# A gated convolution with a mixture of experts on one core: the second unit's weights asked for behind the first rows, and the last group's digits, root and logit differences put between the steps of its ranks

## The chip, the cores and the metric

The kernel runs on one core of one Trainium2 chip. The metric is the device time of one execution in microseconds (us). Before the change three runs took 562.46, 561.94 and 562.39 us, a median of 562.39. An execution was also profiled; all rows of the trace below are from that one.

The names of the engines in the profile: PE is TensorE (matmuls; PEld its weight loads), DVE is VectorE, ACT is ScalarE, POOL is GpSimd, SP is SyncE, which issues most DMA transfers. A trailing q (SPq) marks what an engine's sequencer issues.

## What is computed

```python
def reference(A_q, A_k, A_v, A_shift_k, A_ssm_k, A_ssm_D, B_x, B_wg, B_w1, B_w2):
    x = A_q                                           # 1 x 2048 x 512
    h = x + _A_ref(_layernorm(x), A_k, A_v, A_shift_k, A_ssm_k, A_ssm_D)
    return h + _B_ref(_layernorm(h), B_wg, B_w1, B_w2)

def _B_ref(x, wg, w1, w2):                            # 8 experts, one for each token
    gates = _softmax(xt @ wg)
    topk_idx = jnp.argsort(-gates, -1)[:, :1]
    topk_g = gate of that expert, divided by itself
    h = _gelu(jnp.einsum("nd,edf->nef", xt, w1))      # w1: 8 x 512 x 1792
    y = jnp.einsum("nef,efd->ned", h, w2)             # w2: 8 x 1792 x 512
    return sum over experts of (its weight) * y
```

`_A_ref` is a short and a long causal convolution per channel (the long one by a Fourier transform), with gates. Only the expert that a token chose is computed.

## The kernel before

**Phase 1** makes h, in 16 groups of 128 tokens, writes its rows to `hrow` in memory, and routes: logits, the chosen expert of each token, and the token's rank in its expert. The routing goes in four groups g of 4 times 128 tokens. For each: `pick_steps` (the greatest logit, a one-hot `ohe`, counts `cum`), `rank_own` (two matmuls), `rank_steps` (six dependent instructions on DVE that give the rank and its slot), `route_slots` (one-hot rows `oneb` of the slots), `val_digits` (mean and inverse deviation of a token cut in three bf16 digits `dig`, by four instructions), `rank_select` (`sel`), `route_digits` (`rhs`, the digits times `sel`) and `index_digits` (`rhsj`). `route_list(g)` are the matmuls that sort the digits into lists by slot (`pi`), `route_index` those that sort the row numbers.

**The hand-over to phase 2** is `last_rows`, then `last_group` (group 3), then lines 1762 to 1773. The expert with the most tokens so far, the leader, is computed first; it is known from the first three groups (`leader_steps`, its number in `whol`). Its rows come in three tiles: tile 0 of 128 rows from the first three groups (row numbers `idxa`), tiles 1 (128) and 2 (56 used) behind group 3 (row numbers `idxe`). `gather_rows` (L912) fetches a tile from `hrow` by an indirect DMA on POOL. `first_center` (L973) subtracts the mean and scales on DVE (`xf`), `turn` in `first_in` transposes on PE (L987, `px`), ACT casts to `xh`, DVE takes the rest `xl`, and `multiply` (L1001) starts the first layer: xh by w0h, xh by w0l, xl by w0h, for tile 0 and the first half of the unit's columns, then the rest (128x184), then the second half (128x312).

**Weights.** A unit j is 256 of an expert's 1792 inner columns, 7 units to an expert. `weight_load(j, (0,))` asks SP for its block of w1 (512 KB, L881), `weight_load(j, (1,))` for that of w2 (L884); `weight_cast` (ACT, L899) and `weight_sub` (DVE, L905) split it into w0h, w0l or w1h, w1l. `phase2` puts loads behind a small transfer `seen` (L1445) that reads one row of a gathered tile, and so waits on SP until the tile has landed: the first group of loads behind tile 0, the second behind tile 1.

**What sets the order.** Each engine runs its instructions in program order; in this part the order is written out by hand. `weave` takes one step of each list in turn. Semaphores make an engine wait for another. `spin` (L483, counts in `SPIN`) issues matmuls on a tile of ones that nobody reads; keys c, d, e, f, h, i stand in this part. `values_load` (L876) reads a number from memory into SP's registers, and checks its bounds there unless told not to.

Of the kernel before, what the change touches and what calls it, by code (L numbers as in the profile page):

```python
# [15 lines left out]
AF = mybir.ActivationFunctionType  # L16
# [5 lines left out]
P = 128  # L22
# [59 lines left out]
PAIRS = (1, 3, 5, 7, 9, 11, 13, 15)  # L82
SPLIT = PAIRS[:6]
POOLED = (0, 2, 4, 6, 8, 10)
SPIN = dict(s=24, g=8, a=12, f=14, i=3, h=3, c=12, d=3, e=5)


LAGS = dict(A=0, T=2, L=4)
# [40 lines left out]
class Kernel:  # L129
# [595 lines left out]
    def leader_steps(self):  # L725
        nc, rp = self.nc, self.rp
        key = rp.tile([P, E], F32, name="keyl")
        yield nc.vector.scalar_tensor_tensor(key, self.pl0, float(E), self.tie, op0=ALU.mult, op1=ALU.add)
        top = self.top
        yield nc.vector.tensor_reduce(top, key, axis=AX.X, op=ALU.max)  # L730
        self.lead = rp.tile([P, E], F32, name="lead")
        yield nc.vector.tensor_tensor(self.lead, key, top.to_broadcast([P, E]), op=ALU.is_equal)
        yield nc.vector.tensor_tensor(self.leadp, key, top.to_broadcast([P, E]), op=ALU.is_equal)
        rows = self.lead_rows(0, 12)
        yield next(rows)
        who = rp.tile([P, E], F32, name="whol")
        yield nc.vector.tensor_mul(who, self.lead, self.iotp[:, :E])
        yield next(rows)
        at = rp.tile([P, 1], F32, name="at")
        yield nc.vector.tensor_reduce(at, who, axis=AX.X, op=ALU.add)  # L740
        self.whol = rp.tile([P, 1], I32, name="wholi")
        yield nc.vector.tensor_scalar_sub(self.whol, at, 1.0)

    def route_list(self, g):
        nc, one, rhs = self.nc, self.oneb[:, 4 * g:4 * g + 4], self.rhs[g]
# [47 lines left out]
    def route_exp(self):  # L793
        nc = self.nc
        lg = self.lg
        nc.vector.tensor_sub(lg[:, 12:], self.plg[3][:, :, 0], self.bc(self.mx[:, 12:]))
        nc.vector.tensor_mul(lg, lg, self.val[:, :, 2].unsqueeze(2).to_broadcast([P, N2, E]))

    def route_weights(self):
        nc, rp, lg, mx = self.nc, self.rq, self.lg, self.mx  # L800
# [71 lines left out]
    def weight_load(self, j, parts=(0, 1)):  # L872
        nc = self.nc
        e, c = divmod(j, NJ)
        if c == 0 and 0 in parts:
            self.eid = nc.values_load(self.who[0:1, e:e + 1] if e else self.whol[0:1, 0:1], engines=[mybir.EngineType.SP],  # L876
                                      min_val=0, max_val=E - 1)
        w1, w2 = self.w1[ds(self.eid, 1)], self.w2[ds(self.eid, 1)]
        if 0 in parts:
            r = self.rawt[j, 0] = self.raw.tile([P, DC, FB * P], F32, name="raw1")  # L880
            nc.sync.dma_start(r, w1.rearrange("o (p b) f -> p (o b) f", p=P)[:, :, c * FB * P:(c + 1) * FB * P])  # L881
        if 1 in parts:
            r = self.rawt[j, 1] = self.raw.tile([P, FB, D], F32, name="raw2")
            nc.sync.dma_start(r, w2.rearrange("o (b p) d -> p (o b) d", p=P)[:, c * FB:(c + 1) * FB, :])  # L884
# [91 lines left out]
    def first_in(self):  # L976

        nc = self.nc
        hi, lo = self.xt[0] = self.split(self.xp, self.ident, "x", 2, [P, DC, CAPS[0]])
        tiles = self.first_tiles()  # L980
        ps = [self.px.tile([P, 512], F32, name="px").rearrange("p (c n) -> p c n", c=DC) for _ in tiles][::-1]

        def turn(t):
            n = tiles[t].stop - tiles[t].start
            xv = self.xs[t].rearrange("p (d c) -> p c d", c=DC)
            for b in range(DC):
                nc.tensor.transpose(ps[t][:, b, :n], xv[:n, b, :], self.ident[:n, :n])  # L987
            nc.scalar.copy(hi[:, :, tiles[t]], ps[t][:, :, :n])

        def low(t):  # L990
            n = tiles[t].stop - tiles[t].start
            nc.vector.tensor_sub(lo[:, :, tiles[t]], ps[t][:, :, :n], hi[:, :, tiles[t]].bitcast(F32))

        self.plt = [self.pl1.tile([P, 512], F32, name=f"pl{f}", bufs=1) for f in range(FB)]
        pl = [p[:, :CAPS[0]] for p in self.plt]
        wh, wl = self.wt[0, 0]

        def multiply(s, f, i):
            w, x = ((wh, hi), (wl, hi), (wh, lo))[i]
            for b in range(DC):  # L1000
                nc.tensor.matmul(pl[f][:, s], w[:, b, f * P:(f + 1) * P], x[:, b, s],  # L1001
                                 start=i + b == 0, stop=i == 2 and b == DC - 1)

        rest = slice(P, CAPS[0])
        turn(0)
        self.slot_consts()
        self.spin("e", self.pd)
        self.first_center(2)
        low(0)
        multiply(tiles[0], 0, 0)  # L1010
        multiply(tiles[0], 0, 1)
        turn(1)
        turn(2)
        multiply(tiles[0], 0, 2)
        self.weight_cast(1, 0)
        self.weight_cast(0, 1)
        low(1)
        low(2)
        for i in range(3):
            multiply(rest, 0, i)  # L1020
        for i in range(3):
            multiply(slice(0, CAPS[0]), 1, i)
        return pl
# [306 lines left out]
    def last_rows(self):  # L1330
# [29 lines left out]
        self.rank_sum(2)  # L1360
        self.logits(14)
        weave(self.leader_steps(), self.rank_steps(2))
        for j in range(2):
            self.weight_load(j, (0,))
        self.route_slots(2, dve)
        self.index_digits(1, pool)
        self.route_digits(1, pool)
        self.val_digits(2, pool)
        self.logits(15)

    def last_group(self):
# [6 lines left out]
        self.spin("a", self.psT)  # L1378
        self.ahead_index()
        self.lead_index(0, 12)  # L1380
        self.rank_select(2)
        self.index_digits(2, pool)
        next(pick)
        next(pick)
        self.ahead_rows()
# [4 lines left out]
            self.tc.add_manual_dep(ready.ins, x.name, mybir.DependencyInfo(mybir.DependencyClass.Sync, mybir.DependencyReason.DATA),  # L1390
                                   reason="rows kept and read before they are gathered")
        self.first = [self.gather_rows(self.xp, self.idxa, P)]
        self.route_digits(2, pool)
        self.rank_own(3)
        self.spin("f", self.psT)
        weave(self.rank_steps(3), self.lead_rows(12, N2))
        self.route_slots(3, dve, 0, 2)
        self.lead_digits(12, N2)
        self.route_slots(3, dve, 2, 4)
        self.lead_index(12, N2)  # L1400
        self.ahead_digits()
        self.lead_rows_index()
        self.first_gather()
        self.spin("i", None)
        self.ahead_values()
        self.spin("h", None)
        self.route_scale(3)
        self.val_digits(3, dve, range(1))
        self.route_exp()
        nc.scalar.activation(self.lg, self.lg, AF.Exp)  # L1410
        nc.scalar.activation(self.warm, self.eps, AF.Gelu_apprx_tanh)
        self.val_digits(3, dve, range(1, 4))
        self.rank_select(3)
        self.route_list(1)
        self.route_list(2)
        self.route_digits(3, dve)
        self.index_digits(3, dve)
        self.spin("c", None)
        self.route_list(3)
        self.route_index()  # L1420
        self.hp.release()
        self.open_weights()
        self.weight_cast(0, 0)

    def open_experts(self):
        tc, R = self.tc, self.RIGHT
# [13 lines left out]
    def phase2(self):  # L1440
        nc, tc = self.nc, self.tc
        self.spin("d", self.pd)
        for t, units in enumerate((((0, 1),), ((2, 0), (1, 1), (2, 1), (3, 0), (3, 1), (4, 0), (4, 1)))):
            seen = tc.dram_tile([1, D], F32, name=f"seen{t}")
            gate = nc.sync.dma_start(seen, self.first[t][0:1])  # L1445
            with tc.issue_after(gate.ins):
# [380 lines left out]
```

## Time and profile before

| what | us |
|---|---|
| median of three runs | 562.39 |
| the profiled execution, device time | 561.27 |
| its span, first to last instruction | 559.3 |
| PE busy in the span | 547.8 |
| DVE busy | 450.3 |
| ACT busy | 342.9 |
| POOL busy | 261.7 |
| last steps of the routing and first rows, about | 205 to 224 |

Times in the trace are us from the span's start. In a timeline a row is start, duration, engine, line, operation, result<-inputs, shapes and a count; brackets hold the idle time of the engine before it, and what ended that. A row of the view of waits is total us, times, longest. A row of the view by stretches is busy share (instructions) of PE, PEld, DVE, ACT and POOL, the granted clock of TensorE, the busy share of the DMA engines, and GB/s.

### The profile page before, as it was taken

The numbers are of one execution on the slowest core, as the hardware profiler recorded it, in microseconds if no ns is written. First come the engines' busy times: TensorE is split into PE (matmuls) and PEld (weight loads), VectorE is DVE, ScalarE is ACT, GpSimd is POOL, SyncE is SP. The second block draws the span as 40 slices with busy tenths as digits, with TensorE's granted clock in tenths as the row PEclk, the third lists the DMA queues.
The fourth block names the chain that finished last, engine by engine and source line by source line (L and its number), as shares of the span: only waits on it lengthen the run. The fifth ranks groups of instructions, "written<-read, shape, count | busy, mean of one in ns | idle before, by whom it ended". The sixth has DMA issues, their size and how long they took to land. (4 is left out here: it accounts for less than half of the span.)

```text
span 559.3 us, 10976 instructions
## 1 busy us (share of the span) xinstructions
PE 547.8 (98%) x3753; PEld 471.3 (84%) x3754; DVE 450.3 (81%) x839; ACT 342.9 (61%) x577; POOL 261.7 (47%) x264
## 2 busy tenths in 40 slices
PE   8999999999999998999999999999999999999995
PEld 7857675766556787999999999999999999898984
DVE  5886977889989798878987789899788788786751
ACT  2485667644677753765656566667667667666651
POOL 1055425711367783065574868456457367300201
PEclk9999999999999999999999999999999999999998
DMA  8964559485502326998665767687687778776401
GB/s 320 367 180 179 152 172 377 130 298 154 148 1 94 111 99 181 331 254 297 184 189 169 227 191 217 185 242 232 202 232 211 228 213 284 226 226 200 156 2 38
DMA packets 62674, 110.49 MB, mean 198 GB/s; under 512 B 6142, under 2 KB 36226, under 8 KB 60216
## 3 DMA queue, kind: packets, MB, share of 16 engines
q1 hardware_dynamic: 57622, 98.74, 57.0%
q0 software_dynamic: 4816, 10.43, 5.6%
q8 instruction: 64, 1.05, 0.8%
q14 instruction: 26, 0.21, 0.1%
q10 hardware_dynamic: 146, 0.05, 0.0%
HBM read 91.76 MB, written 13.68 MB: 189 GB/s over the span
## 5 line engine op out<-in xcount | busy, mean ns | idle before, releaser
L945 POOL DMA_INDIRECT hq<-hrow,ix x61 | 75.8, 1242 | 85.2 <-DVE ix L942 69.7
L899 ACT CAST w1h<-raw 128x1024 fp32r<-128x1024 f32 x56 | 58.7, 1050 | 47.1 <-PE py L1132 33.1
L1110 ACT ACTIVATE g<-pl 128x312 f32<-128x312 f32 (+7 forms) x112 | 44.5, 398 | 63.2 <-PE pl L1097 54.5
L905 DVE TENSOR_TENSOR w1l<-raw,w1h 128x1024 fp32r<-128x1024 f32 x56 | 68.8, 1229 | 17.1 <-ACT w1h L899 16.9
L1132 PE MATMUL py<-gsh,w1h 128*128 128x312 f32 (+4 forms) x280 | 80.9, 289 | 0.3 <-issue 0.3
L1132 PE MATMUL py<-gsl,w1h 128*128 128x312 f32 (+4 forms) x280 | 80.7, 288 | 0.0
L1132 PE MATMUL py<-gsh,w1l 128*128 128x312 f32 (+4 forms) x280 | 80.7, 288 | 0.0
L905 DVE TENSOR_TENSOR w0l<-raw,w0h 128x1024 fp32r<-128x1024 f32 x56 | 69.0, 1232 | 13.3 <-ACT w0h L899 12.9
L1115 DVE TENSOR_TENSOR gsl<-g,gsh 128x312 fp32r<-128x312 f32 (+7 forms) x112 | 50.5, 452 | 32.7 <-ACT gsh L1111 30.4
L1149 POOL DMA_INDIRECT out_dram<-yq,idxq x47 | 62.5, 1329 | 24.5 <-DVE yq L1177 12.0
L1097 PE MATMUL pl<-xh,w0h 128*128 128x240 f32 (+5 forms) x440 | 71.0, 283 | 0.0
L1097 PE MATMUL pl<-xl,w0h 128*128 128x240 f32 (+5 forms) x440 | 70.8, 283 | 0.0
L1097 PE MATMUL pl<-xh,w0l 128*128 128x240 f32 (+5 forms) x440 | 70.8, 283 | 0.0
L1097 PEld LDWEIGHTS pl<-xh,w0h 128*128 128x128 f32 x440 | 61.8, 189 | 1.7
L1097 PEld LDWEIGHTS pl<-xl,w0h 128*128 128x128 f32 x440 | 60.4, 189 | 0.0
L1097 PEld LDWEIGHTS pl<-xh,w0l 128*128 128x128 f32 x440 | 60.4, 189 | 0.0
L899 ACT CAST w0h<-raw 128x1024 fp32r<-128x1024 f32 x56 | 58.5, 1044 | 0.0
L254 POOL TENSOR_TENSOR zs<-zs,spec 128x512 f32<-128x512 f32 x32 | 39.9, 1273 | 35.2 <-ACT zs L253 35.2
L1132 PEld LDWEIGHTS py<-gsh,w1h 128*128 128x128 f32 x280 | 52.6, 188 | 0.6 <-issue 0.5
L1132 PEld LDWEIGHTS py<-gsh,w1l 128*128 128x128 f32 x280 | 52.7, 188 | 0.0
L1132 PEld LDWEIGHTS py<-gsl,w1h 128*128 128x128 f32 x280 | 52.7, 188 | 0.0
L1111 ACT CAST gsh<-g 128x312 fp32r<-128x312 f32 (+7 forms) x112 | 47.1, 420 | 3.6
(295 smaller groups left out, 1083.4 us busy)
## 6 DMA issues: line engine op xcount, KB each, us to landing
raw<-B_w SPq DMA_DIRECT2D x112, 512.0 KB, 4.4
spec<-spec SPq DMA_DIRECT2D x64, 128.0 KB, 2.3
kt<-A_ssm_k SPq DMA_DIRECT2D x4, 1024.0 KB, 6.0
vv<-A_v SPq DMA_DIRECT2D x4, 1024.0 KB, 15.1
kT<-A_k SPq DMA_DIRECT2D x3, 1216.0 KB
kT<-A_q SPq DMA_DIRECT2D x2, 1024.0 KB, 8.3
hrow<-kT SPq DMA_DIRECT2D x8, 256.0 KB, 2.2
fa<-c_fa SPq DMA_DIRECT2D x1, 1024.0 KB, 13.3
```

What stands on the lines that cost most here:

```text
L254: nc.gpsimd.tensor_mul(zs, zs, self.spec[:, 1, W * h:W * h + W])
L899: self.nc.scalar.copy(h, r)
L905: self.nc.vector.tensor_sub(o, r, h.bitcast(F32))
L945: self.last_gather = nc.gpsimd.indirect_dma_start(out=self.hq[e][:, lo + i, :], out_offset=None, in_=rows, in_offset=bass.IndirectOffsetOn ...
L1097: nc.tensor.matmul(ps[:, :n], w[:, b, f * P:(f + 1) * P], x[:, b, :n], start=k == 0, stop=k == 3 * DC - 1)
L1110: nc.scalar.activation(g, ps, AF.Gelu_apprx_tanh)
L1111: nc.scalar.copy(ghi[:, f, :], g)
L1115: self.nc.vector.tensor_sub(glo[:, f, :], self.g[f], ghi[:, f, :].bitcast(F32))
L1132: nc.tensor.matmul(y[b][:, :size], wv[:, b, f], g[:, f, :size], start=st and i == 0, stop=sp and i == 2)
L1149: st = nc.gpsimd.indirect_dma_start(out=out, out_offset=bass.IndirectOffsetOnAxis(ap=idx, axis=0), in_=o, in_offset=None, bounds_check=out ...
```

## The change

Four things are edited. The load of unit 1's first weights leaves `last_rows` and stands behind the first `seen`. Of group 3, `route_scale`, the first digit step and the two steps of `route_exp` (now a generator) stand ahead of the ranks; the second and third digit step are woven into the rank steps; the exponential and the load of the next function table on ACT follow. `rank_select(2)`, `index_digits(2)` and `route_digits(2)` come earlier, and the lists of groups 1 and 2 ahead of those of group 3. The fillers c and d are 3 and 8 instead of 12 and 3. In `first_in` the turns of tiles 1 and 2 come ahead of the second product, and the leader's number is kept at zero or above, without the check of its bounds.

```diff
-SPIN = dict(s=24, g=8, a=12, f=14, i=3, h=3, c=12, d=3, e=5)
+SPIN = dict(s=24, g=8, a=12, f=14, i=3, h=3, c=3, d=8, e=5)
...
         yield nc.vector.tensor_reduce(at, who, axis=AX.X, op=ALU.add)
+        yield self.rank_select(2)
         self.whol = rp.tile([P, 1], I32, name="wholi")
-        yield nc.vector.tensor_scalar_sub(self.whol, at, 1.0)
+        yield nc.vector.tensor_scalar(self.whol, at, 1.0, 0.0, op0=ALU.subtract, op1=ALU.max)
...
     def route_exp(self):
...
-        nc.vector.tensor_sub(lg[:, 12:], self.plg[3][:, :, 0], self.bc(self.mx[:, 12:]))
-        nc.vector.tensor_mul(lg, lg, self.val[:, :, 2].unsqueeze(2).to_broadcast([P, N2, E]))
+        yield nc.vector.tensor_sub(lg[:, 12:], self.plg[3][:, :, 0], self.bc(self.mx[:, 12:]))
+        yield nc.vector.tensor_mul(lg, lg, self.val[:, :, 2].unsqueeze(2).to_broadcast([P, N2, E]))
...
-            self.eid = nc.values_load(self.who[0:1, e:e + 1] if e else self.whol[0:1, 0:1], engines=[mybir.EngineType.SP],
-                                      min_val=0, max_val=E - 1)
+            self.eid = nc.values_load(
+                self.who[0:1, e:e + 1] if e else self.whol[0:1, 0:1], engines=[mybir.EngineType.SP], min_val=0, max_val=E - 1,
+                skip_runtime_bounds_check_because=None if e else "the maximum of eight places less one, not under zero")
...
         multiply(tiles[0], 0, 0)
-        multiply(tiles[0], 0, 1)
         turn(1)
         turn(2)
+        multiply(tiles[0], 0, 1)
         multiply(tiles[0], 0, 2)
...
         weave(self.leader_steps(), self.rank_steps(2))
-        for j in range(2):
-            self.weight_load(j, (0,))
+        self.weight_load(0, (0,))
...
         self.val_digits(2, pool)
+        self.index_digits(2, pool)
+        self.route_digits(2, pool)
         self.logits(15)
...
         self.lead_index(0, 12)
-        self.rank_select(2)
-        self.index_digits(2, pool)
         next(pick)
...
         self.first = [self.gather_rows(self.xp, self.idxa, P)]
-        self.route_digits(2, pool)
+        exps = self.route_exp()
+        self.route_scale(3)
+        next(exps)
+        self.val_digits(3, dve, range(1))
+        next(exps)
         self.rank_own(3)
         self.spin("f", self.psT)
-        weave(self.rank_steps(3), self.lead_rows(12, N2))
+        self.route_list(1)
+        self.route_list(2)
+        weave(self.rank_steps(3), self.last_steps())
+        nc.scalar.activation(self.lg, self.lg, AF.Exp)
+        nc.scalar.activation(self.warm, self.eps, AF.Gelu_apprx_tanh)
         self.route_slots(3, dve, 0, 2)
         self.lead_digits(12, N2)
         self.route_slots(3, dve, 2, 4)
         self.lead_index(12, N2)
+        self.val_digits(3, dve, range(3, 4))
+        self.rank_select(3)
         self.ahead_digits()
         self.lead_rows_index()
         self.first_gather()
         self.spin("i", None)
         self.ahead_values()
         self.spin("h", None)
-        self.route_scale(3)
-        self.val_digits(3, dve, range(1))
-        self.route_exp()
-        nc.scalar.activation(self.lg, self.lg, AF.Exp)
-        nc.scalar.activation(self.warm, self.eps, AF.Gelu_apprx_tanh)
-        self.val_digits(3, dve, range(1, 4))
-        self.rank_select(3)
-        self.route_list(1)
-        self.route_list(2)
         self.route_digits(3, dve)
+        self.route_list(3)
         self.index_digits(3, dve)
         self.spin("c", None)
-        self.route_list(3)
         self.route_index()
...
+    def last_steps(self):
+        lists = self.lead_rows(12, N2)
+        dig = (self.val_digits(3, self.nc.vector, range(i, i + 1)) or True for i in (1, 2))
+        for x in (lists, dig, lists, dig, lists):
+            yield next(x)
...
-        for t, units in enumerate((((0, 1),), ((2, 0), (1, 1), (2, 1), (3, 0), (3, 1), (4, 0), (4, 1)))):
+        for t, units in enumerate((((1, 0), (0, 1)), ((2, 0), (1, 1), (2, 1), (3, 0), (3, 1), (4, 0), (4, 1)))):
```

On DVE, between the row numbers of tiles 1 and 2 (`idxe`) and the digit lists of group 3 (`rhs`), before:

```order
L697 TENSOR_REDUCE idxe<-pY 128x2
L552 RECIPROCAL val<-val 128x4
L538 CAST dig<-val 128x8
L796 TENSOR_TENSOR lg<-plg,mx 128x32
L797 TENSOR_TENSOR lg<-lg,val 128x128
L540 TENSOR_TENSOR digr<-val,dig 128x8
L542 CAST dig<-digr 128x8
L544 TENSOR_TENSOR dig<-digr,dig 128x8
L624 TENSOR_TENSOR sel<-ohe,pc 128x96
L653 TENSOR_TENSOR rhs<-sel,dig 128x576
```

The same engine now, from the counts `cum` of group 3 to the slot `lo`; `rk`, `rank`, `ge`, `lo` are the rank steps (lines from 744 on stand one or two later than before):

```order
L581 SCALAR_TENSOR_TENSOR cum<-pc,ohe 128x32
L552 RECIPROCAL val<-val 128x4
L797 TENSOR_TENSOR lg<-plg,mx 128x32
L538 CAST dig<-val 128x8
L798 TENSOR_TENSOR lg<-lg,val 128x128
L611 TENSOR_TENSOR rk<-pY,ohe 128x32
L668 TENSOR_TENSOR olm<-ohe,pc 128x32
L613 TENSOR_REDUCE rank<-rk 128x4
L540 TENSOR_TENSOR digr<-val,dig 128x8
L615 TENSOR_TENSOR ge<-rank,pc 128x12
L669 TENSOR_REDUCE pc<-olm 128x4
L617 TENSOR_REDUCE pc<-ge 128x4
```

Four of the eight instructions stand ahead of `rk` now, and two between the rank steps (the second is `L542 CAST`, right behind these rows); the last two come just ahead of `idxe`, and `rhs` follows `idxe` at once.

On SP, from the leader's number on (raw is a block of weights, frow a copy of the gathered rows), before:

```order
L876 TENSOR_LOAD wholi
L876 ISA x2
L881 ISA
L881 DMA raw_2058<-B_w 128x4x256
L881 ISA
L881 DMA raw_2060<-B_w 128x4x256
L1445 DMA seen_2313<-row 1x512
L884 ISA
L884 DMA raw_2315<-B_w 128x2x512
L926 DMA frow<-row 128x512
L1445 DMA seen_2317<-row 1x512
```

and now:

```order
L877 TENSOR_LOAD wholi
L883 ISA
L883 DMA raw_2052<-B_w 128x4x256
L1453 DMA seen_2300<-row 1x512
L883 ISA
L883 DMA raw_2302<-B_w 128x4x256
L886 ISA
L886 DMA raw_2304<-B_w 128x2x512
L928 DMA frow<-row 128x512
L1453 DMA seen_2306<-row 1x512
```

Unit 1's block (raw_2060, now raw_2302) has moved behind the first `seen`, ahead of unit 0's block of w2; the two bookkeeping instructions of the check are gone.

On PE, from the first product that uses the low half of the weights (w0l) or of the rows (xl), before (px is the turn of a row tile, pl a product's bank; xh and xl are the two halves of the rows):

```order
L1001 MATMUL pl_2338<-xh,w0h 128x128 x4
L1001 MATMUL pl_2338<-xh,w0l 128x128 x4
L987 MATMUL px<-ident,xf 128x128 x4
L987 MATMUL px<-ident,xf 128x56 x4
L1001 MATMUL pl_2338<-xl,w0h 128x128 x4
L1001 MATMUL pl_2338<-xh,w0h 128x184 x4
```

and now, from the same first product (lines are two later):

```order
L1003 MATMUL pl_2327<-xh,w0h 128x128 x4
L989 MATMUL px<-ident,xf 128x128 x4
L989 MATMUL px<-ident,xf 128x56 x4
L1003 MATMUL pl_2327<-xh,w0l 128x128 x4
L1003 MATMUL pl_2327<-xl,w0h 128x128 x4
L1003 MATMUL pl_2327<-xh,w0h 128x184 x4
```

The turns of the second and third tile now stand straight behind the first product, and the product with w0l behind them.

## The prediction

> **What bounds the kernel now.** I read the page first, for who is busy over the whole span, and then the waits of TensorE (PE) alone from 223 us to the end.
>
> ```profile
> span 559.3 us, 10976 instructions
> PE 547.8 (98%) x3753; PEld 471.3 (84%) x3754; DVE 450.3 (81%) x839; ACT 342.9 (61%) x577; POOL 261.7 (47%) x264
> ```
>
> ```profile
> PE py L1132 <- issue: 0.3, 1, 0.3
> ```
>
> The second fence is the whole answer for 223 to 560 us: in 336 us PE waits once, for 0.3 us. So everything behind 224 us is a dense stream of PE work, and the change, all of whose edits lie in front of that, can only shift the start of the stream. The question is therefore one of a few us. The third view is PE's timeline where the stream begins (start, duration, instruction, idle time before it in brackets).
>
> ```profile
> 217.20 1.47 PE L483 MATMUL pT<-ones 128*128 128x256 bf16 x12
> 218.61 0.41 PE L747 MATMUL pi<-rhs,oneb 128*128 128x144 bf16 x4
> 218.86 0.56 PE L660 MATMUL pY<-rhsj,oneb 128*128 128x48 bf16 x16
> ...
> 219.32 0.49 PE L483 MATMUL pT<-ones 128*128 128x256 bf16 x3
> 220.29 0.72 PE L987 MATMUL px<-ident,xf 128*128 128x128 f32 x4 [0.48 <-DVE xf L973]
> ...
> 221.68 0.66 PE L1001 MATMUL pl<-xh,w0h 128*128 128x128 f32 x4
> ...
> 222.63 1.33 PE L987 MATMUL px<-ident,xf 128*128 128x128 f32 x8
> 223.89 0.66 PE L1001 MATMUL pl<-xl,w0h 128*128 128x128 f32 x4
> 224.39 0.69 PE L1001 MATMUL pl<-xh,w0h 128*128 128x184 f32 x4
> ```
>
> L483 is filler whose result nobody reads; that PE looks busy there is no evidence. The real chain is: the list matmul L747, the first rows centred on VectorE (DVE, xf), turned on PE (px, L987), and from 221.68 on no gap: each row starts where the one before makes room. I measure everything at the 128x184 product, at 224.39; what it gains the kernel gains. The same chain on DVE:
>
> ```profile
> 213.23 0.19 DVE L611 TENSOR_TENSOR rk<-pY,ohe 128x32 f32<-128x32 f32 x1 [0.29 <-PE pY L601]
> ...
> 215.92 0.16 DVE L697 TENSOR_REDUCE idxe<-pY 128x2 int32<-128x4 f32 x1 [0.16 <-PE pY L712]
> ...
> 216.21 0.18 DVE L538 CAST dig<-val 128x8 bf16<-128x8 f32 x1
> ...
> 216.91 0.42 DVE L542 CAST dig<-digr 128x8 bf16<-128x8 f32 x1
> ...
> 217.80 0.76 DVE L653 TENSOR_TENSOR rhs<-sel,dig 128x576 bf16<-128x576 f32 x1
> ...
> 219.60 0.54 DVE L973 TENSOR_SCALAR xf<-row,sv 128x512 f32<-128x512 f32 x1
> ...
> 221.38 0.98 DVE L973 TENSOR_SCALAR xf<-row,sv 128x512 f32<-128x512 f32 x2
> ```
>
> **The change, part by part.** *Digits, root and differences moved forward.* Between the row index idxe (215.92) and the digit lists rhs (217.80) stand the eight instructions that move: 1.9 us. In their new place they lie partly in the 0.29 us that DVE waits for PE before the ranks, and partly between rank steps that each wait for the one before. Some still cost time there. Bounds: nothing, or what the first four took alone, about 0.7 us (216.0 to 216.7 on the same rows), less the 0.29, so 0.4. I take 0.1 and let idxe stand at 216.0 and rhs at 216.1, 1.7 us earlier. Everything from L747 to the first xf follows it: xf at 217.9 in place of 219.60.
>
> *Fillers.* PE, with the list matmul at 216.9, has 3 fillers left there where 12 stood, then L660 and 8 fillers where 3 stood. Twelve took 1.41 us (217.20 to 218.61), so one is 0.12 at most: 216.9 + 0.25 + 0.35 + 0.46 + 0.94 = 218.9. The first turn would have its data at 218.6 (0.69 behind xf, as before). The fillers, not the data, then end last: px at 218.85, a gain of 1.45 here, not 1.7.
>
> *The exponential and the table load* go forward with the differences; ScalarE (ACT) then casts the first weights as soon as they land instead of behind the load.
>
> ```profile
> 218.45 0.20 ACT L1411 ACTIVATE warm<-eps 128x1 f32<-128x1 f32 x1
> ...
> 223.38 0.96 ACT L988 CAST xh<-px 128x512 fp32r<-128x512 f32 x2 [1.24 <-PE px L987]
> ```
>
> I cost both at nothing: the weights of unit 0 are asked for at 212.20 or a little earlier (two bookkeeping instructions of SyncE go) and take 4.3 us, so their cast ends by 217.6, ahead of the first product at 220.25. The turns put ahead of the second product give ACT its input 0.47 us sooner; in before that cast ended at 224.34, just in time for 224.39, so this earns nothing itself, but it puts px 1 and px 2 straight behind the first product, with no PE work left to cover a late row.
>
> *Weights of the second unit behind the first rows.* Here the queues decide: SyncE (SPq, issue time and issue duration), its waits, the landing time of the weights asked for first, GpSimd (POOL, the gathers with the writing of their descriptors), and the DMA rate in stretches of 1 us (the last number, GB/s).
>
> ```profile
> 212.20 1.48 SPq L881 DMA_DIRECT2D raw<-B_w  x2
> 218.63 0.30 SPq L1445 DMA_DIRECT2D seen<-row  x1
> 219.12 0.44 SPq L884 DMA_DIRECT2D raw<-B_w  x1
> ...
> 220.59 0.24 SPq L1445 DMA_DIRECT2D seen<-row  x1
> ```
>
> ```profile
> SPq L1445 <- DMA row<-hrow,idxa: 4.9, 1, 4.9
> ...
> SPq L1445 <- DMA row<-hrow,idxe: 0.4, 1, 0.4
> ```
>
> ```profile
> raw<-B_w SPq DMA_DIRECT2D x1, 512.0 KB, 4.3
> ```
>
> ```profile
> 213.54 1.19 POOL L912 DMA_INDIRECT row<-hrow,idxa  x1 [0.58 <-DVE olm L668]
> ...
> 216.37 0.99 POOL L912 DMA_INDIRECT row<-hrow,idxe  x1 [0.44 <-DVE val L552]
> 217.66 0.91 POOL L912 DMA_INDIRECT row<-hrow,idxe  x1 [0.30 <-issue]
> ```
>
> ```profile
> 213.00:214.00 1.00, 1.00 (x11) 0.90 (x11) 0.74 (x6) 0.00 (x0) 0.46 (x1) 1.00 0.36 30
> 214.00:215.00 1.00, 0.73 (x7) 0.40 (x5) 0.79 (x5) 0.00 (x0) 0.96 (x2) 1.00 0.72 211
> 215.00:216.00 1.00, 0.51 (x7) 0.49 (x8) 0.84 (x5) 0.00 (x0) 0.92 (x1) 1.00 1.09 386
> 216.00:217.00 1.00, 1.00 (x23) 0.95 (x21) 0.90 (x7) 0.17 (x1) 0.64 (x1) 1.00 1.09 383
> 217.00:218.00 1.00, 1.00 (x14) 0.92 (x12) 0.86 (x4) 0.98 (x2) 0.70 (x2) 1.00 0.94 318
> ```
>
> By 217.0 these stretches have moved 1.01 MB, which is both weight blocks (1.05 MB); the first row tile is seen only at 218.63, 5.1 us behind its gather. So I read that what was asked for first went first: the second block, issued from about 213.0, held up rows whose descriptors were only written by 214.73. Without it, 512 KB at 386 GB/s, 1.36 us, drop out ahead of the rows: they land at about 217.2, in time for xf at 217.9. That makes the 1.7 usable; without this edit xf would wait until 218.6.
>
> The block now starts 0.49 us behind the first "seen" (218.63 to 219.12), at about 217.7. There it meets the gathers of the other two row tiles, which the change doesn't move: they hang on idxe, and are issued near 216.4 and 217.7, the last with its descriptors written by 218.6. The second tile is written before 217.7 and should land as before, at 220.55 (SyncE waited 0.4 for it, to 220.59). The third, 128 KB, would stand behind the block as the first tile did: 217.7 + 4.3 + 128 KB at 386 GB/s (0.33) = 222.3. Centring takes about 0.5, the turn of the third tile 0.63 (half of 222.63 to 223.89), the two products now behind it 0.47 and 0.50: 222.3 + 0.5 + 0.63 + 0.97 = 224.4. That is where it stands now. Bounds for the third tile: 220.9, from the spacing of the two gathers and 220.55 less the half size, and 223.6, if a second block goes ahead too.
>
> *The port of DVE and GpSimd.* The cast of 0.42 us above began inside the gather at 216.37 and ended with it, at 217.33 against 217.36, while the same cast at 216.21 took 0.18. The cast now stands near 214.2, where the first gather writes; at worst it is held to 214.73, 0.5 us on the rank chain. The Trainium skill, SBUF — State Buffer, Practical consequences, says that a cast in a two-port mode and GpSimd exclude each other, whoever starts first; the row agrees, and by that rule the sum would carry 0.5 us on idxe, by the free cast nothing.
>
> **The sum.** Third tile behind the block: the 128x184 product at 224.35 against 224.39, no change worth naming. The profiled execution took 561.27 us, its span 559.3; the median of the runs is 562.39, 1.1 above it, and I add the shift to the median: **562.3**, its own range 561.8 to 562.9.
>
> **The rivals.** *A, the third tile isn't held up.* Then the second tile at 220.55 ends last: xf to 221.1, turn to 221.8, the third turn to 222.45, two products to 223.4: 1.0 us gained, 561.4. If the second tile lands sooner too, the fillers bound it: 1.45 gained, 560.9. For it: the block may be issued after 218.6, when the descriptors stand. Against: 217.7 is what the rows give. A rule of the DMA engines would bring it about as well, if they took turns between the queues: the third tile would share the rate with the block, land near 221.2 and gain 0.9. The first tile speaks against it, since it got no share while two blocks moved. The Trainium skill, DMA: Bandwidth & Descriptors, Queues, rings and completion order, states such turns, packet by packet.
>
> *B, slower: two blocks go ahead of the third tile.* Unit 0's second weights (219.12 in before) now follow the block at once, near 218.4, just ahead of 218.6. If they too are served first, 1.36 us are added: 562.3 + 1.3 = 563.6. It decides at whether that issue comes before the last descriptors; the first tile's block was 0.5 us ahead of its gather's start, this one would be 0.7 behind it, which speaks against it.
>
> *C, the forward move doesn't come off:* DVE is held at the cast and idxe moves to 216.4, so that both row tiles follow: 0.4 on the sum, 562.7.
>
> **How the numbers follow.** Forecast 0.50, A 0.27 (0.20 by a later issue or earlier rows, 0.07 by turns between the queues), B 0.13, C 0.10. A measurement of this kernel can tell about 0.2%, 1.1 us, from no change. A lies half beyond that on the fast side, and the forecast's fast edge adds a little: faster 0.19. B lies beyond it for the most part: slower 0.12. Same: 0.69. The range takes in A whole and B up to near its price: 560.9 to 563.5.
>
> **What would show it.** L653 near 216.1, the first xf near 217.9 and px near 218.85 show the move right. The first "seen" near 217.2 and the next raw near 217.7 show the queue right. The idle time before the second and third px decides between forecast and A; a third tile seen behind 223 is B. It would be wrong if PE waits again behind 224 us, for weights that now come later, or if its granted clock, 1.00 in all rows above, falls where the turns wait with no filler.

## The result, and the profile after

| | before | after |
|---|---|---|
| median (lowest to highest of 5) | 562.38 us (561.94 to 562.46) | 568.32 us (567.58 to 569.73) |
| profiled execution, its span | 561.27, 559.3 | 567.58, 565.8 |
| mean granted clock of TensorE | 0.997 | 0.991 |

The ratio is 1.0114, with a 95% interval of 1.0096 to 1.0132: the change costs 5.4 to 7.4 us. The forecast was 562.3, within 560.9 to 563.5, and slower had a chance of 0.12.

The cores view of the changed kernel, and the one wait of over half a microsecond in its list of PE's waits from 213 to 235 us (line that waits, what it waits for, total, times, longest):

```profile
core 0: 565.8 us, clock 0.991
```

```profile
PE px L989 <- DVE xf L975: 3.4, 1, 3.4
```

Before the change PE waited 0.48 us at that line, for the first row tile. Now it waits 3.4 us at one instruction. The table by stretches, of two microseconds each (length, then busy time of PE, PEld, DVE, ACT and POOL with counts, then the granted clock, the share of the DMA engines and GB/s):

```profile
222.00:224.00 2.00, 0.00 (x0) 0.00 (x0) 0.00 (x0) 0.59 (x1) 0.00 (x0) 1.00 0.88 274
224.00:226.00 2.00, 0.59 (x4) 0.55 (x4) 1.18 (x3) 0.00 (x0) 0.00 (x0) 0.61 1.06 380
226.00:228.00 2.00, 2.00 (x11) 1.93 (x10) 1.45 (x3) 1.82 (x3) 0.00 (x0) 0.50 1.07 405
228.00:230.00 2.00, 2.00 (x11) 2.00 (x11) 1.99 (x5) 0.41 (x1) 0.00 (x0) 0.50 1.06 382
230.00:232.00 2.00, 2.00 (x13) 2.00 (x12) 0.54 (x4) 0.88 (x2) 0.00 (x0) 0.68 1.08 370
232.00:234.00 2.00, 2.00 (x17) 2.00 (x16) 0.41 (x2) 1.21 (x3) 0.00 (x0) 1.00 1.09 376
```

PE does nothing from 222 to 224 and little up to 226. Behind that the granted clock is 0.50, up to about 231. In the kernel before it was 1.00 in every one of these stretches; two of them, before the change:

```profile
224.00:226.00 2.00, 2.00 (x18) 2.00 (x19) 1.67 (x3) 2.00 (x3) 0.00 (x0) 1.00 1.02 335
226.00:228.00 2.00, 2.00 (x16) 2.00 (x16) 1.99 (x7) 1.28 (x4) 0.00 (x0) 1.00 1.04 398
```

So the change costs twice: PE stands still, and when it goes on it runs at half its clock. DMA isn't idle meanwhile: it moves 274 and 380 GB/s.

The timeline shows what it moves. Rows of the changed kernel (start, duration, engine, line; in brackets the idle time ahead of the row and what ended it); SPq is SyncE asking for a transfer, and the duration of the gather on POOL is read here as the time in which GpSimd writes its descriptors, the orders by which the DMA engines move the rows:

```profile
216.54 0.75 DVE L653 TENSOR_TENSOR rhs<-sel,dig 128x576 bf16<-128x576 f32 x1
...
216.91 1.22 POOL L914 DMA_INDIRECT row<-hrow,idxe  x1 [2.38 <-DVE idxe L697]
...
217.82 0.30 SPq L1453 DMA_DIRECT2D seen<-row  x1
...
218.33 0.58 SPq L883 DMA_DIRECT2D raw<-B_w  x1
218.33 0.56 DVE L975 TENSOR_SCALAR xf<-row,sv 128x512 f32<-128x512 f32 x1
...
218.43 0.91 POOL L914 DMA_INDIRECT row<-hrow,idxe  x1 [0.30 <-issue]
...
219.10 0.47 SPq L886 DMA_DIRECT2D raw<-B_w  x1
...
219.25 0.64 PE L989 MATMUL px<-ident,xf 128*128 128x128 f32 x4
...
220.58 0.24 SPq L1453 DMA_DIRECT2D seen<-row  x1
...
224.82 0.54 DVE L975 TENSOR_SCALAR xf<-row,sv 56x512 f32<-56x512 f32 x1 [3.63 <-DMA row<-hrow,idxe]
...
225.41 0.73 PE L989 MATMUL px<-ident,xf 56*128 56x56 f32 x4 [3.42 <-DVE xf L975]
...
227.83 1.10 PE L1003 MATMUL pl<-xh,w0h 128*128 128x184 f32 x4
```

The first tile is read at 218.33 (xf), 1.27 us earlier than before, and its turn is at 219.25 instead of 220.29. Up to there the change does what it says. The third tile's gather starts at 218.43 and its descriptors are written at 218.43 + 0.91 = 219.34. Ahead of that moment SyncE has asked for two blocks of 512 KB: the second unit's w1 at 218.33 and the first unit's w2 at 219.10. The tile's xf starts at 224.82, where DVE had waited 3.63 us for the DMA. That is 6.4 us behind the gather's start; before the change it landed 3.2 us behind it (gather at 217.66, last completion at 220.90; in the trace a transfer completes in sixteen parts, and it has landed with the last), with no block asked for in between: the w2 block came at 219.12, and the descriptors had been written at 218.57. The 128x184 product, 224.39 before, stands at 227.83.

### The profile page after: what moved, and what is told of

Same layout as the page of the kernel before. It is cut to its first block, busy times and chain, and to the rows that moved or that the text cites. A ratio compares the mean times of both kernels' runs of the same rounds, so it can differ in the third digit from the quotient of the medians.

```text
span 565.8 us, 10965 instructions
## 1 busy us (share of the span) xinstructions
PE 550.2 (97%) x3749; PEld 473.6 (84%) x3750; DVE 450.5 (80%) x839; ACT 343.3 (61%) x577; POOL 262.4 (46%) x264
```

## The experiments

Four kernels share a chip in each of three groups. A group's ratios are against runs of the kernel before on the same chip, since that differs (564.12, 562.41 and 562.59 us in the three). A ratio is worked out from all these runs and need not be the quotient of the medians. Each edit is shown against the changed kernel, where nothing else is said.

### First group: which part costs the time

Without the queue move (the second unit's block asked for at once, as before the change; the rest of the change stays):

```
-        self.weight_load(0, (0,))
+        for j in range(2):
+            self.weight_load(j, (0,))
...
-        for t, units in enumerate((((1, 0), (0, 1)), ((2, 0), ...
+        for t, units in enumerate((((0, 1),), ((2, 0), ...
```

> The changed kernel with the second unit's block of w1 asked for at once again, as before the change; all other parts of the change stay. Theory H (the third row tile stands behind that block in the DMA queues, PE runs out of work for 3.4 us, and its clock is halved after that): the third tile lands near 221.3 again, PE waits under 1 us ahead of its turn, the clock stays at 1.00, and the time is 561.0 to 563.0. Rival R (the moved digits, the later rank chain and the order of the turns cost the time, wherever the block stands): 565 or more.

Measured: 567.32 us, ratio 1.0039 (1.0011 to 1.0068), with twelve times from 561.76 to 569.55. Neither theory foresaw such a spread. The times go with the mean granted clock: 561.8 and 562.1 us at 0.998, 565.2 to 565.9 at 0.994, 567.2 to 567.9 at 0.991 or 0.992, and 569.1 to 569.6 at 0.988. The profiled execution took 567.89; its timeline:

```profile
218.72 0.91 POOL L914 DMA_INDIRECT row<-hrow,idxe  x1 [0.30 <-issue]
...
219.43 0.43 SPq L886 DMA_DIRECT2D raw<-B_w  x1
...
224.02 0.54 DVE L975 TENSOR_SCALAR xf<-row,sv 56x512 f32<-56x512 f32 x1 [2.44 <-DMA row<-hrow,idxe]
...
224.61 0.68 PE L989 MATMUL px<-ident,xf 56*128 56x56 f32 x4 [2.22 <-DVE xf L975]
```

The second unit's block is long out of the way here, and the third tile is late all the same: 5.3 us behind its gather's start. The block in front is now w2, asked for at 219.43; the descriptors were written by 219.63. In the trace the sixteen DMA engines complete their parts of the tile from 221.29 to 224.00, where they take 220.25 to 220.90 in the kernel before: some parts were held for long, others hardly. So theory H named the wrong thing, a certain block. The next theory, H2: whatever is asked for before the gather's descriptors are written goes ahead of its rows. Here the two moments are 0.20 us apart, which would fit a tile that is held in some executions and not in others; only one execution was profiled, so that isn't shown.

The queue move alone, in the kernel before:

```
-        for j in range(2):
-            self.weight_load(j, (0,))
+        self.weight_load(0, (0,))
...
-        for t, units in enumerate((((0, 1),), ((2, 0), ...
+        for t, units in enumerate((((1, 0), (0, 1)), ((2, 0), ...
```

> The kernel before with one edit: the second unit's block of w1 stands behind the first tile's check, ahead of the first unit's block of w2. Nothing else of the change. Theory H: the third tile lands between 222.5 and 225, PE waits 1.5 to 3.5 us ahead of its turn, and the time is 564 to 569. Rival R: 561.5 to 563.

Measured: 564.65 us, ratio 1.0013 (1.0000 to 1.0025). The block was asked for 0.41 us ahead of the end of the descriptors, w2 0.37 behind it, and the tile landed 4.5 us behind its gather's start, at 222.79. But PE did not wait for it: without the moved digits the first xf starts only at 220.85, and the first tile's turn was what PE waited for (0.5 us). The held tile hid behind that. So theory H missed the wait of 1.5 us or more, and its time of 564 to 569 came out only because the kernel before takes 564.12 on this chip. The queue move by itself costs nearly nothing. Two things differ in the changed kernel: the earlier digits bring PE to the third tile sooner, and the tile is held for longer (6.4 us), with w2 ahead as well.

All weights behind the check of the second row tile:

```
-        for t, units in enumerate((((1, 0), (0, 1)), ((2, 0), (1, 1), ...
+        for t, units in ((1, ((1, 0), (0, 1), (2, 0), (1, 1), ...
```

> The changed kernel with all weights after the first block behind the check of the second row tile; the check of the first tile falls away. Theory H: nothing large is asked for until about 220.6, when the third gather's descriptors have long been written; the third tile lands near 221.2, the 128x184 product stands at 223 to 224, the clock stays at 1.00, and the time is 560.5 to 562.5. Rival: the first unit's w2 and the second unit's w1 now come 2 us later and PE waits for them behind 224: 563 to 566. Rival R: 565 or more.

Measured: 564.74 us, ratio 1.0012 (0.9995 to 1.0028). The clock is at 1.00 in the profile, with 0.9 us of waits for row tiles. The tile landed 4.1 us behind its gather's start: SyncE now had nothing ahead of the copy of the first rows (256 KB) and asked for it at 217.98, before the descriptors of either later gather were written (218.28 and 219.56). The rival of the expectation, that the weights now come later, may show besides: PE waits 0.8 us for ACT's g at 228.90. So this is not a clean trial of H2.

Fillers in the wait:

```
+SPIN = dict(..., x=26)
...
         turn(1)
+        self.spin("x", self.pd)
         turn(2)
```

> The changed kernel with 26 filler products (128x256 bf16, 0.12 us each, 3.1 us) between the turns of the second and the third row tile; the wait for the third tile stays. If the halved clock is a price of its own, brought about by the idle PE: the clock stays at 1.00 from 224 to 232 and the time falls by 1.0 to 2.2 us against the changed kernel, to 566 to 567.3. If the clock falls for another reason, or costs nothing beside the wait: 567.5 to 569.5.

Measured: 565.76 us, ratio 1.0032 (1.0015 to 1.0049), clock 1.00 throughout. The tile lands 6.4 us behind its gather's start, as in the changed kernel. The changed kernel wasn't on this chip, so the price of the clock is read in the third group.

### Second group: is it the end of the descriptors that decides?

A memset on GpSimd behind the last gather, and the second unit's block waits for it (to keep the queue's order, the copies of the rows are asked for behind the block):

```
         self.first += [self.gather_rows(...) ...]
+        self.written = self.nc.gpsimd.memset(self.held, 0.0).ins
...
+            dma = nc.sync.dma_start(r, w1...)
+            if j == 1:
+                self.tc.add_manual_dep(dma.ins, self.written.name, ...)
+                self.behind = dma.ins
...
+            with self.tc.issue_after(self.behind):
                 nc.sync.dma_start(rows[t * P:t * P + n], r[:n])
```

> The changed kernel, with the second unit's block (and what follows it on SyncE) made to wait until GpSimd has written the third gather's descriptors, by a memset behind that gather; the copies of the rows are asked for behind that block. Theory H2 (what is asked for before the third gather's descriptors are written goes ahead of its rows, whichever block it is): the block is asked for 0.1 to 0.5 us behind the end of that writing, the third tile lands 3.2 to 4.2 us behind its gather's start instead of 6.4, PE waits under 1.2 us for its turn, the clock stays at 1.00, and the time is 3 to 6 us under the changed kernel, 1 us to either side of the kernel before. Rival R2 (the tile is late because weights move beside it, whoever was asked first): it lands 5 us or more behind its gather's start, and the time stays 2 us or more above the kernel before.

Measured: 562.56 us, ratio 1.0016 (0.9996 to 1.0037), clock 0.998. Its timeline (lines four to six later):

```profile
219.06 0.91 POOL L918 DMA_INDIRECT row<-hrow,idxe  x1 [0.30 <-issue]
...
219.97 0.12 POOL L925 MEMSET held<- 128x1 f32 x1
220.11 0.59 SPq L883 DMA_DIRECT2D raw<-B_w  x1
...
222.24 0.54 DVE L981 TENSOR_SCALAR xf<-row,sv 56x512 f32<-56x512 f32 x1 [0.45 <-DMA row<-hrow,idxe]
...
222.83 0.69 PE L995 MATMUL px<-ident,xf 56*128 56x56 f32 x4 [0.23 <-DVE xf L981]
```

The block is asked for at 220.11, 0.14 us behind 219.06 + 0.91 = 219.97, and the tile is there at 222.24, 3.2 us behind its gather's start. PE's wait is 0.23 us. R2 as it was put falls, for it had 5 us or more whoever was asked first. But the block's own parts land only from 223.68 on, and the tile's by 222.22, so the two hardly moved side by side any more. The run shows that a later asking frees the tile; by what rule the DMA engines choose between two transfers it doesn't show. The twelve times still spread from 560.76 to 567.13, the three longest at a mean clock of 0.991 to 0.993.

The same wait for the w2 block, in the kernel with the second unit's block asked for at once (the edit above with `if j == 0` at w2, on top of the first run of the first group):

> The changed kernel with the second unit's block asked for at once, as before the change, and the first unit's block of w2 made to wait for the third gather's descriptors as in the run beside it. H2: the third tile lands 3.2 to 4.2 us behind its gather's start (5.3 without the wait), the times lie together within 2 us where they were spread over 8, and the median is within 1 us of the kernel before. R2: spread and 2 us or more above the kernel before.

Measured: 563.56 us, ratio 1.0024 (1.0005 to 1.0043). The tile lands 3.5 us behind its gather's start instead of 5.3, and PE's two waits for row tiles make 0.5 us. The times, 561.07 to 566.24, lie closer than without the wait (7.8 us) but not within 2 us: a miss on that count, and the median is 1.15 us above the kernel before, just beyond what was expected.

Now the kernel **before**, with nothing of the change, and its third gather made late:

```
+        for t in range(1, -(-CAPS[0] // P)):
+            self.first.append(self.gather_rows(...))
+            for _ in range(12 if t == 1 else 0):
+                self.nc.gpsimd.memset(self.held, 0.0)
```

> The kernel before with twelve memsets of one column on GpSimd between the second and the third gather, so that the third gather's descriptors are written about 0.8 to 1.2 us later, behind the asking for the first unit's block of w2. Nothing else is changed. H2: the third tile is held by that block, lands 4.5 us or more behind its gather's start, at 223 to 225, and the time is 1.5 to 5 us above the kernel before. R2, or a tile that is only as late as its gather: it lands 3.2 to 3.6 us behind its start, near 222, PE waits 0.5 us or less, and the time is within 0.7 us of the kernel before.

> The kernel of the run beside it, with the same twelve memsets, and the block of w2 (and what follows on SyncE, the row copies last) made to wait until the third gather's descriptors are written. H2: the third tile lands 3.2 to 4.2 us behind its gather's start though that start is as late, and the time is within 1 us of the kernel before, below the run beside it. R2: no difference from the run beside it.

The second of the two runs has the same memsets and adds the wait, as in the runs above. Timeline of the first of them, without a wait for the descriptors:

```profile
218.04 1.84 POOL L920 MEMSET held<- 128x1 f32 x12
...
219.74 0.44 SPq L884 DMA_DIRECT2D raw<-B_w  x1
...
220.02 0.91 POOL L912 DMA_INDIRECT row<-hrow,idxe  x1
...
225.22 0.54 DVE L975 TENSOR_SCALAR xf<-row,sv 56x512 f32<-56x512 f32 x1 [2.72 <-DMA row<-hrow,idxe]
```

and of the second, where w2 waits for them (and the row copies come last):

```profile
220.32 0.90 POOL L916 DMA_INDIRECT row<-hrow,idxe  x1
...
221.22 0.12 POOL L925 MEMSET held<- 128x1 f32 x1
221.37 0.44 SPq L884 DMA_DIRECT2D raw<-B_w  x1
...
223.20 0.54 DVE L981 TENSOR_SCALAR xf<-row,sv 56x512 f32<-56x512 f32 x1 [0.39 <-DMA row<-hrow,idxe]
```

The memsets took 1.84 and 1.83 us, more than meant. Without the wait w2 is asked for at 219.74, the descriptors are written at 220.93, the tile comes 5.2 us behind its gather's start, the clock falls to 0.50, and the time is 567.32 us, ratio 1.0080 (1.0060 to 1.0100). Here the order of asking was kept in full: the first part of the tile landed at 224.70, behind the last of w2 at 223.87. With the wait w2 is asked for 0.15 us behind the descriptors, the tile comes 2.9 us behind its gather's start, and the time is 562.86, ratio 1.0007 (0.9994 to 1.0020), although that gather starts 0.3 us later still. This pair makes and unmakes nearly the whole loss in a kernel without the change: 4.5 us between them. The copy of the first rows (256 KB), asked for at 220.23 without the wait, moved behind the descriptors along with w2, so the pair stands for both.

### Third group: the price of the clock, and two versions

> The changed kernel as it is, as the measure for the three runs beside it on the same chip. By H2 the third tile lands 5 us or more behind its gather's start, PE waits 2 us or more for its turn, the clock falls behind 224 us, and the time is 3 to 7 us above the kernel before.

> The changed kernel with 26 filler products between the turns of the second and the third tile, now beside the changed kernel on one chip. If the halved clock has a price of its own: 1.0 to 3.0 us under the changed kernel, with the third tile as late as there. If not: within 0.7 us of it.

The changed kernel: 568.56 us, ratio 1.0113 (1.0096 to 1.0130), the tile 6.4 us behind its gather's start. With fillers (the same kernel as in the first group): 565.15, ratio 1.0041 (1.0025 to 1.0058), the tile 6.6 us behind. The stretches of the changed kernel, and then those with fillers (columns as above):

```profile
222.00:224.00 2.00, 0.54 (x4) 0.34 (x3) 0.00 (x0) 0.59 (x1) 0.00 (x0) 0.99 0.81 220
224.00:226.00 2.00, 0.00 (x0) 0.00 (x1) 0.59 (x2) 0.00 (x0) 0.00 (x0) 0.50 1.03 373
226.00:228.00 2.00, 2.00 (x11) 1.90 (x11) 1.53 (x3) 1.24 (x3) 0.00 (x0) 0.50 1.08 398
228.00:230.00 2.00, 2.00 (x11) 2.00 (x11) 1.91 (x2) 1.00 (x2) 0.00 (x0) 0.50 1.05 395
230.00:232.00 2.00, 2.00 (x10) 2.00 (x10) 0.74 (x5) 0.70 (x2) 0.00 (x0) 0.50 1.08 365
232.00:234.00 2.00, 2.00 (x10) 2.00 (x9) 0.48 (x1) 0.18 (x1) 0.00 (x0) 0.50 1.08 367
```

```profile
222.00:224.00 2.00, 2.00 (x21) 1.79 (x19) 0.00 (x0) 0.59 (x1) 0.00 (x0) 1.00 0.84 238
224.00:226.00 2.00, 1.28 (x12) 0.93 (x10) 0.86 (x2) 0.00 (x0) 0.00 (x0) 1.00 1.03 365
226.00:228.00 2.00, 2.00 (x19) 1.94 (x18) 1.45 (x4) 1.54 (x3) 0.00 (x0) 1.00 1.07 400
228.00:230.00 2.00, 2.00 (x18) 2.00 (x17) 2.00 (x2) 1.58 (x3) 0.00 (x0) 1.00 1.06 382
```

Without fillers the clock is 0.50 up to 234 us, with them it stays at 1.00. The difference, 3.4 us (4 runs against 9), is the price of the halved clock, a little over what was expected. The other 2.6 us above the kernel before are put down to the wait: the versions without it, below, are within 0.5 us of the kernel before.

The block behind the descriptors with four memsets instead of one (SyncE's check of the second tile kept behind the block), and the same with the product with w0l ahead of the turns of the second and third tile, as before the change:

```
-        self.written = self.nc.gpsimd.memset(self.held, 0.0).ins
+        for _ in range(4):
+            self.written = self.nc.gpsimd.memset(self.held, 0.0).ins
...
+        multiply(tiles[0], 0, 1)
         turn(1)
         turn(2)
-        multiply(tiles[0], 0, 1)
```

> The changed kernel with the block behind the third gather's descriptors, as in the earlier run of that kind, but with four memsets instead of one, so that it is asked for 0.5 to 0.9 us behind the end of that writing (the kernel before: 0.55) instead of 0.14. If the order at the DMA engines is decided with some jitter around the end of the writing, the margin takes away the late runs: times within 2.5 us of each other and a median 0.2 to 1.2 us under the kernel before. If the spread has another source: times as wide as with the short margin (6 us) and a median within 0.5 us of the kernel before.

> The run beside it with one edit: the product of the first tile with the low half of the weights (w0l) stands ahead of the turns of the second and third tile again, as before the change. If the new order of the turns is worth what the prediction took, 0.1 us or less either way: within 0.5 us of the run beside it. If the later turns let PE run without a wait for the third tile: 0.2 to 0.5 us faster.

The first: 562.15 us, ratio 1.0010 (0.9991 to 1.0030), times 560.75 to 565.85. Its timeline:

```profile
218.40 0.91 POOL L918 DMA_INDIRECT row<-hrow,idxe  x1 [0.30 <-issue]
...
219.31 0.58 POOL L926 MEMSET held<- 128x1 f32 x4
...
219.92 0.59 SPq L883 DMA_DIRECT2D raw<-B_w  x1
...
221.69 0.54 DVE L982 TENSOR_SCALAR xf<-row,sv 56x512 f32<-56x512 f32 x1 [0.43 <-DMA row<-hrow,idxe]
```

With 0.61 us of margin the tile takes 3.3 us, about as with 0.14 us (3.2). The spread is still 5.1 us (3.2 in the kernel before), so jitter at the end of the writing isn't its source. The clock goes with it: the four late times, 564.17 to 565.85 us, have a mean granted clock of 0.992 to 0.995, the other seven 0.997 to 0.999. Why it fell in those four stays open, since the one profile is of an execution of 561.81 us. The second: 562.95 us, ratio 1.0004 (0.9991 to 1.0018), PE without a wait for the tile. Its median is 0.8 us above that of the run beside it, where 0.5 at most was expected, but the intervals overlap, and in time the order of the turns makes no difference that can be told. In the clock it may: none of its twelve runs is below 0.997, while with the turns of the second and third tile early 4 of 11 are here, and 5 of 12 with one memset. No run was made to test that. Neither version is faster than the kernel before.

### All of them side by side

"Ahead" counts the transfers of 512 KB asked for before the third gather's descriptors were written (gather's start plus its duration); "lag" is from the start of that gather to the tile's last completion in the trace. Each number is from one profile.

| kernel | first block asked for, against the end of the descriptors | ahead | lag, us |
|---|---|---|---|
| before | 0.55 behind | 0 | 3.2 |
| w2 behind them, gather late | 0.15 behind | 0 | 2.9 |
| w1 behind them; with margin; old turns | 0.14; 0.61; 0.60 behind | 0 | 3.2; 3.3; 3.1 |
| early block, w2 behind them | 0.29 behind | 0 | 3.5 |
| queue move alone | 0.41 ahead | 1 | 4.5 |
| early block | 0.20 ahead | 1 | 5.3 |
| before, gather late | 1.19 ahead | 1, and the row copy (256 KB) | 5.2 |
| changed, two profiles | 1.01; 1.08 ahead | 2 | 6.4; 6.4 |
| changed with fillers, two profiles | 0.95; 1.19 ahead | 2 | 6.4; 6.6 |

None ahead: 2.9 to 3.5 us. One: 4.5 to 5.3. Two: 6.4 to 6.6. (The run behind the second tile's check, with 256 KB of row copy ahead, gave 4.1.) So asking ahead of the end of the descriptors delays the tile, and asking behind it doesn't.

A price for each block isn't shown. The middle of the sixteen parts doesn't follow the count: it lands 2.7 to 2.9 us behind the gather's start with none ahead, 3.5 to 5.0 with one, 3.7 to 4.9 with two. In the changed kernel 13 of the tile's parts had landed by 223.38, before the first part of w2 at 224.23, though w2 was asked for 0.24 us ahead; only the last parts, for which xf waits, came late. And no run has w1 as far ahead as there with w2 behind the descriptors, so the second block's own share stays open.

## Why the prediction was wrong

**The digits between the steps: right.** The first xf gained 1.27 us where 1.7 were forecast. At L567, long before the change's effect, this execution already runs 0.32 us later than the one of before (206.42 against 206.10), so the gain is about 1.6. The turn at 219.25 against a forecast of 218.85 is that same shift and little else.

**The first tile held by the second block: right, but for less.** Without that block it landed at 217.80 (218.61 before), and the first check stood at 217.82 instead of 218.63, where 217.2 was forecast. Over the profiles the check stands 5.0 to 5.5 us behind the first gather's start with that block asked for early (five), 4.1 to 4.6 without (eight): about 0.9 us on average, not 1.36.

**Two small misses on the third gather.** The forecast left it at 217.7; it came at 218.43. Of the 0.77 us, 0.32 are the general shift. Another 0.23 is the second gather's length: 1.22 us where it took 0.99. L653 now runs beside it (216.54 to 217.29), and the gather ends 0.84 us behind that. In the ten profiles with L653 at this place it takes 1.22 us, in the four with L653 where it stood before 0.99. No run tests L653 apart; if the two exclude each other, the forecast had this in view for the digit cast and not for the product that the change pulls to the gather. The rest is the rank chain, 0.2 us longer with the digits in it. Rival C, the cast held at the first gather, didn't happen: L542 stands at 214.65, just behind that gather's end at 214.53, and takes 0.17 us.

**The step that failed: "The third, 128 KB, would stand behind the block as the first tile did".** It was to land at 222.3 and landed at 224.79. That a transfer asked for earlier holds the rows was right, and the forecast used it for one block. It had to decide on the second block, w2, and did so by the wrong moment: "the first tile's block was 0.5 us ahead of its gather's start, this one would be 0.7 behind it, which speaks against it". The start doesn't decide. In the run with the early block, w2 came 0.71 us behind the gather's start and 0.20 ahead of the end of its descriptors, and the tile was held. In the run with w2 behind them, 0.29 us past that end, it wasn't. By the end, the forecast's own figures (w2 near 218.4, descriptors by 218.6) met rival B's condition, and B was given only 0.13. In the run w2 and the end of the descriptors both came 0.7 us later than forecast; that w2 still stood ahead, by 0.24 us, was chance. What the runs show in the step's place: with both blocks ahead the tile lands 6.4 us behind its gather's start, with none 2.9 to 3.5. How much of that is the second block's stays open, as said above.

**B's price was low.** It took 1.36 us for the second block. From its gather's start the tile took 6.4 us where the forecast's sum has 4.6 (217.7 to 222.3), so 1.8 more, and with the gather 0.7 us behind the forecast it landed 2.5 late. And B ended at 563.6, because it counted the wait alone.

**A bound that doesn't come out.** The forecast's 220.9 for a third tile that isn't held is the completion of the kernel before (220.90), but not the sum that it names: 220.55 and the 1.3 us between the gathers, less the 0.33 for 128 KB, make 221.5.

**What no term held: the clock.** A wait of this length was in B, and the prediction's last sentence named the granted clock as what would make it wrong, but put no price on it. The fillers show 3.4 us, more than half of the loss of 5.9.

**Taking turns: not as that rival had it.** The Trainium skill, DMA: Bandwidth & Descriptors, Queues, rings and completion order, has the engines go round between the queues packet by packet; by that the forecast had the third tile share the rate with the block and land near 221.2. It landed at 224.79, and in the late gather's run no part of it landed before the whole of w2 had, which speaks for the order of asking. But strict order doesn't fit the changed kernel, where most of the tile came ahead of w2. By what rule the engines choose stays open.

## What to carry to other kernels

In these runs a gather on GpSimd is held by what SyncE asks for before its descriptors are written (0.20 us ahead of that moment did harm, 0.14 behind it none), not only by what comes before its start: compare that moment with each large transfer that SyncE asks for, and hold those back by a wait on GpSimd if the rows are urgent. Where two changes each pull work forward, ask what they reach together: here the earlier check let two blocks in ahead of a gather that hadn't moved forward. And price an idle TensorE above its wait, since the clock may fall behind it.

## What was unexpected of the hardware

The clock fell after short pauses. In the run with the early block PE was idle for 2.2 us, up to 224.61, and its stretches of one microsecond read:

```profile
223.00:224.00 1.00, 0.00 (x0) 0.00 (x0) 0.00 (x0) 0.01 (x1) 0.00 (x0) 1.00 1.04 382
224.00:225.00 1.00, 0.39 (x3) 0.39 (x4) 0.98 (x2) 0.00 (x0) 0.00 (x0) 1.00 1.03 325
225.00:226.00 1.00, 1.00 (x10) 0.94 (x9) 1.00 (x3) 0.67 (x2) 0.00 (x0) 0.97 1.07 340
226.00:227.00 1.00, 1.00 (x7) 1.00 (x6) 0.45 (x2) 1.00 (x2) 0.00 (x0) 0.50 1.04 392
...
232.00:233.00 1.00, 1.00 (x6) 1.00 (x5) 0.00 (x0) 0.57 (x2) 0.00 (x0) 0.62 1.08 354
```

The clock fell near 226, more than a microsecond after PE had gone on, and was full again near 232. In the late gather's run a pause of 1.9 us did the same, and in the two profiles of the changed kernel behind pauses of 3.4 and 3.5 us the clock was halved for 6.8 and 10.2 us. Waits of up to 1.0 us (the longest in the first run with fillers) left it at 1.00. In the trace's record of the clock the four stretches at 0.50 last 6.82, 6.83, 6.83 and 10.24 us, two or three times 3.41. The Trainium skill, TensorE: Matmul & The Clock Gate, Part 1: The HAM clock gate, names an idle window of about 3.4 us; here pauses of 1.9 and 2.2 us were enough.
